# Score units taken in steps of two or three, with one sum and one reciprocal for each step

## The chip, the cores and the metric

One core of a Trainium2 chip runs the whole program. The metric is the device time of one execution in microseconds (us), lower is better. The engines are TensorE (PE in the rows; its weight loads are PEld), VectorE (DVE), ScalarE (ACT), GpSimd (POOL), and SyncE, whose queue (SP) issues the DMAs.

## The reference

Three blocks follow each other on eight batches of 576 tokens: an attention whose keys and values are pooled by 8, a gated MLP with a product over the sequence, and the block in which the change lies, four attention experts gated by their two best logits:

```python
def _moe2_ref(x, w_gate, wq, wk, wv, wo):      # x: 8 x 576 x 512, 4 experts of width 64
    logits = x @ w_gate
    topk = np.argpartition(-logits, K, axis=-1)[..., :K]          # K = 2
    ...                                                            # w: softmax over the two
    for e in range(E):
        q, k, v = x @ wq[e], x @ wk[e], x @ wv[e]
        scores = scale * (q @ k.transpose(0, 2, 1))
        scores = np.where(causal, -1000000000.0, scores)
        scores = scores - scores.max(-1, keepdims=True)
        a = np.exp(scores)
        a /= a.sum(-1, keepdims=True) + 1e-09
        ye = a @ v @ wo[e]
        ...                                                        # out += mask * w * ye
```

## The kernel before

The first two blocks (class `PhaseA`) take the first 596 us; their code does not change. The second stage (class `PhaseB`) computes the experts for one batch after the other. The four experts of a batch are two pairs `p`; the two experts `e` of a pair share tiles. The queries of a pair are cut into nine **score units** `u`: unit 0 holds the last 64 queries of both experts (`e == 2` in the table `QT`, 576 keys, in two PSUM tiles of 320 and 256 columns), units 1 to 4 are the blocks of 128 queries of the first expert with 512, 384, 256 and 128 keys, units 5 to 8 the same of the second.

A unit passes through these functions. `score`: matmuls into PSUM (L817 to L819, L829, L830), on VectorE the row maximum with the mask (L831; L822 and L824 for unit 0), on ScalarE the exponential, which also writes the row sum (L834). `scale`: on VectorE the sum plus 1e-9 (L845, L843 for unit 0) and its reciprocal (L846), both on one column, then on GpSimd (for a few units of the first and last batch on VectorE) the product of the exponentials with the reciprocal and the gate (L850). `trans`: TensorE transposes the unit (L876, L863 for unit 0), ScalarE copies the high part (L880, L867), VectorE writes the difference (L881, L872). When all units of an expert are transposed, `av` multiplies with the values (L896) in two column groups, ScalarE and VectorE fold the halves (L900, L901), and for the second expert of a pair split the result into `ah` and `al` (L906, L907), which `outp` (L918 to L920) multiplies with the output weights.

The order is written out by hand in `run`. At unit k the program issues `score(k)`, `scale(k-1)`, then the **fill** of that place, then `trans(k-3)` (`LAG = 3`), with `av` ahead of the `trans` once an expert is complete. The fill tables (`FILL`, `FIRSTF` for the first batch, `LASTF` for the last) name other work by short words: `10 11 12 13` are the four projections of pair two (two halves of q, two of k; L703 to L705), `00` to `03` those of pair one of the next batch, `v0` to `v4` its values (L757, L771 to L773), `g` its gate, `x0` to `x3` the loads of its input (L629, with casts on VectorE L630 and differences L633, L634), `o0` to `o3` the output products of the batch before. `put_q` and `put_k` copy a projection out of PSUM (L716, L718, L719, L721; L734, L735), and SyncE's queue copies parts of it to other partitions (L727 for q, L741 for k).

A scheduler then orders each engine's instructions by its own costs; the order of an engine is fixed in the program. All PSUM tiles of the stage share eight banks, `bank(name)`, in turn: a matmul into a bank waits until the tile that had it eight tiles ago has been read. Five buffers `pr` hold the exponentials in turn, and `pbh`, `pbl` one pair's transposed units.

Of the kernel before, what the change touches and what calls it, by code (L numbers as in the profile page):

```python
# [603 lines left out]
FIRSTF = (('10', '11', '12', '13', 'x0', '', 'x1 x2', 'x3', ''), ('v0 00', '', '01 02 v1', '03', '', '', '', 'v2 v3', 'v4 g'))  # L604
LASTF = (('', '10 12 11', '', '', '13', '', 'o1', '', 'o0'), ('', '', '', '', '', 'o2', '', '', 'o3'))
XV1 = (2, 3)
# [6 lines left out]
class PhaseB:  # L613
# [191 lines left out]

    def score(self, b, p, u):
        nc, w = self.nc, self.w
        i, e = QT[u]
        qs, qd, qz = self.QK["q", b, p]
        kd, kl = self.QK["k", b, p]  # L810
        st = w.tile([128, 8], F32, name="sm", bufs=4)
        pt = self.pr[:, (18 * b + 9 * p + u) % 5]
        if e == 2:
            parts = []
            for s in (slice(0, 320), slice(320, S)):
                o = self.bank("s4")[:, :s.stop - s.start]
# [5 lines left out]
            nc.vector.tensor_tensor_reduce(o, o, self.ml, -0.125, BIG, OP.add, OP.min, st[:, 4:5])  # L822
            o = parts[0][0]
            nc.vector.tensor_tensor_reduce(o, o, self.mk[:, 0:1].to_broadcast([128, 320]), -0.125, st[:, 4:5],  # L824
                                           OP.add, OP.min, st[:, 0:1])
        else:
            n = 128 * i + 128
            o = self.bank("s")[:, :n]
            nc.tensor.matmul(o, qs[:, e, 128 * i:n], kd[:, e, :n], start=True, stop=False)  # L829
            nc.tensor.matmul(o, qz[e][:, 128 * i:n], kl[:, :n], start=False, stop=True)  # L830
            nc.vector.tensor_tensor_reduce(o, o, self.mk[:, 576 - n:576], -0.125, BIG, OP.add, OP.min, st[:, 0:1])  # L831
# [3 lines left out]
        self.U[b, p, u] = (pt, st)  # L835

    def scale(self, b, p, u):
        nc = self.nc
        i, e = QT[u]
        pt, st = self.U[b, p, u]  # L840
        gw, wl = self.GW[b]
        if e == 2:
            nc.vector.tensor_scalar(st[:, 2:3], st[:, 1:2], 1e-9, st[:, 5:6], op0=OP.add, op1=OP.add)  # L843
        else:
            nc.vector.tensor_scalar(st[:, 2:3], st[:, 1:2], 1e-9, None, op0=OP.add)  # L845
        nc.vector.reciprocal(st[:, 3:4], st[:, 2:3])  # L846
        g = wl[:, p:p + 1] if e == 2 else gw[:, i, 2 * p + e:2 * p + e + 1]
        n = min(S, 128 * i + 128)
        (nc.vector if (p, u) in (SDF if b == 0 else SDL if b + 1 == B else ()) else
         nc.gpsimd).tensor_scalar(pt[:, :n], pt[:, :n], st[:, 3:4], g, op0=OP.mult, op1=OP.mult)  # L850

    def trans(self, b, p, u):
        nc, w = self.nc, self.w
        i, e = QT[u]
        pt, _ = self.U.pop((b, p, u))
        if u == 0:
# [67 lines left out]
    def run(self):  # L924
# [5 lines left out]
        vpart = lambda b: [lambda t=t: self.vproj(b, t) for t in range(NT)]  # L930
        units = [(b, p, u) for b in range(B) for p in range(2) for u in range(9)]
        def item(b, x):
            if x[0] == "x":
# [12 lines left out]
        for x in PRE.split():  # L946
            for f in item(0 if x[0] == "1" else -1, x):
                f()
        for k in range(len(units) + LAG + 1):
            if k < len(units):  # L950
                b, p, u = units[k]
                self.score(b, p, u)
            if 0 <= k - 1 < len(units):
                self.scale(*units[k - 1])
            if k < len(units):
                for x in (LASTF if b + 1 == B else FILL if b else FIRSTF)[p][u].split():
                    for f in item(b, x):
                        f()
            j = k - LAG
            if 0 <= j - 1 < len(units):  # L960
                b_, p_, u_ = units[j - 1]
                if u_ in (5, 8):
                    for g in range(2):
                        self.av(b_, p_, u_ // 8, g)
            if 0 <= j < len(units):
                self.trans(*units[j])
        for f in range(4):
# [38 lines left out]
```

## Time and profile before

| what | value |
| --- | --- |
| median of 3 runs | 986.61 us (985.52 to 988.78) |
| the profiled execution's own time | 986.47 us |
| its span | 984.4 us |
| mean granted TensorE clock | 0.979 |
| TensorE busy, share of the span | 93% |
| VectorE, ScalarE, GpSimd | 73%, 52%, 50% |

The span runs from the first to the last instruction of the profiled execution; about 2 us of its own time lie around it. Busy shares are means over both stages. In the second stage (from about 596 us) a batch repeats with the same pattern, so that stretches of a batch's length tell what a batch costs. A wait in the rows is idle time of an engine in front of an instruction, put down to the work that ended it.

### The profile page before, as it was taken

To read this page: it belongs to the slowest core of one execution; us is meant where nothing else is said; L and a number is where in the kernel's file an instruction comes from. 1 tells how busy PE (TensorE), PEld (TensorE's weight loads), DVE (VectorE), ACT (ScalarE), POOL (GpSimd) and SP (SyncE) were. 2 spreads that over 40 slices of the span, in tenths; PEclk is the share of its full clock that TensorE was granted. 3 is DMA by queue.
4 is the path that set the end of the run, shared out by engine and by line. 5 is a ranking of instruction groups with operands and counts; after the bars stand their busy time and mean duration, and the time that the engine had idled before them with its cause. 6 is when DMAs were issued, how large, how long until landed. Compare 5 with 4: busy or idle time off the path is not lost.

```text
span 984.4 us, 18357 instructions
## 1 busy us (share of the span) xinstructions
PE 915.4 (93%) x6488; PEld 863.3 (88%) x6488; DVE 715.2 (73%) x1901; ACT 511.1 (52%) x1291; POOL 490.4 (50%) x670
## 2 busy tenths in 40 slices
PE   4577899999999999999999999799999999999997
PEld 3366889989989999899899899799999999899987
DVE  6998747757567567476577524998979797979785
ACT  5576334334243343242342433576767676767776
POOL 6863727648369367375584450234434242525221
PEclk9589899999999999999999999999999999999999
DMA  9430321302302304122024012324233323322121
GB/s 331 186 101 22 101 88 47 128 26 81 110 20 71 118 12 141 45 82 99 31 62 121 1 52 70 84 48 118 72 112 72 116 74 96 84 84 84 48 60 73
DMA packets 37819, 82.92 MB, mean 84 GB/s; under 512 B 4960, under 2 KB 11104, under 8 KB 36832
## 3 DMA queue, kind: packets, MB, share of 16 engines
q1 hardware_dynamic: 37584, 81.75, 26.5%
q8 instruction: 52, 0.85, 0.4%
q14 instruction: 39, 0.32, 0.1%
q10 hardware_dynamic: 144, 0.00, 0.0%
HBM read 49.23 MB, written 18.87 MB: 69 GB/s over the span
## 4 chain that ended last, share of the span: by engine, by line
PE 57%; DVE 25%; ACT 8%; POOL 5%; issue 4%; DMA 1%; SPq 0%; POOLq 0%; ACTq 0%; DVEq 0%
PE op L445 4%; PE op L446 3%; PE op L447 3%; PE sp L420 3%; PE sp L422 3%; PE sp L421 3%; PE sc L230 3%; PE av L896 3%; DVE vnl L390 2%; DVE vnh L392 2%; ACT pr L834 2%; PE t L876 2%; PE tr L281 2%; DVE bs L376 2%; PE pj L705 2%
## 5 line engine op out<-in xcount | busy, mean ns | idle before, releaser
L850 POOL TENSOR_SCALAR pr<-pr,sm,gw 128x128 f32<-128x128 f32 (+3 forms) x119 | 77.9, 655 | 157.6 <-DVE sm L846 127.1
L834 ACT ACTIVATE pr<-s,sm 128x256 f32<-128x256 f32 (+4 forms) x160 | 83.0, 520 | 42.0 <-DVE sm L845 17.1
L332 POOL TENSOR_TENSOR xu<-x 128x576 f32<-128x576 f32 x28 | 39.2, 1428 | 98.3 <-DVE x L327 85.4
L446 PE MATMUL op<-g,woh 128*128 128x288 f32 x256 | 76.6, 301 | 4.2 <-POOL g L433 3.8
L420 PE MATMUL sp<-wsh,vnh 128*128 128x288 f32 x256 | 78.4, 306 | 1.6 <-ACT vnh L388 1.6
L404 PE MATMUL up<-x,wih 128*128 128x288 f32 x256 | 76.9, 301 | 2.4 <-ACT vg L364 2.2
L445 PE MATMUL op<-g,woh 128*128 128x288 f32 x256 | 78.2, 308 | 0.0
L421 PE MATMUL sp<-wsh,vnl 128*128 128x288 f32 x256 | 76.1, 297 | 0.0
L422 PE MATMUL sp<-wsl,vnh 128*128 128x288 f32 x256 | 75.9, 297 | 0.0
L406 PE MATMUL up<-x,wil 128*128 128x288 f32 x256 | 75.7, 296 | 0.0
L705 PE MATMUL pj<-xbh,wql 128*128 128x288 f32 x256 | 75.5, 295 | 0.0
L704 PE MATMUL pj<-xbl,wqh 128*128 128x288 f32 x256 | 75.5, 295 | 0.0
L703 PE MATMUL pj<-xbh,wqh 128*128 128x288 f32 x256 | 75.5, 295 | 0.0
L405 PE MATMUL up<-x,wih 128*128 128x288 f32 x256 | 75.1, 293 | 0.0
L447 PE MATMUL op<-g,wol 128*128 128x288 f32 x256 | 75.0, 297 | 0.0
L282 ACT ACTIVATE pth<-tr 128x640 fp32r<-128x640 f32 (+1 forms) x40 | 26.2, 654 | 79.6 <-PE tr L281 70.0
L876 PE MATMUL t<-ident,pr 128*128 128x128 f32 x320 | 57.9, 280 | 9.4 <-POOL pr L850 6.0
L831 DVE CUSTOM_DVE_ANT_0 s<-s,mk 128x512 f32<-128x512 f32 (+3 forms) x128 | 62.5, 488 | 0.4
L881 DVE TENSOR_TENSOR pbl<-t,pbh 128x512 fp32r<-128x512 f32 (+3 forms) x128 | 60.7, 484 | 2.4 <-ACT pbh L880 1.4
L230 PE MATMUL sc<-kbd,qt 128*128 128x144 f32 (+1 forms) x320 | 50.3, 303 | 10.9 <-DMA qt<-q_in 8.5
L361 PE MATMUL vp<-wih,x 128*128 128x512 f32 x128 | 52.0, 406 | 6.2 <-ACT wih L128 5.0
L896 PE MATMUL av<-pbh,vt 128*128 128x320 f32 (+4 forms) x224 | 55.6, 278 | 2.4 <-ACT pbh L880 2.4
(247 smaller groups left out, 3380.3 us busy)
## 6 DMA issues: line engine op xcount, KB each, us to landing
kraw<-k_in SPq DMA_DIRECT2D x16, 576.0 KB, 3.8
x<-x SPq DMA_DIRECT2D x32, 288.0 KB, 2.1
xb<-x SPq DMA_DIRECT2D x32, 288.0 KB, 3.0
kd<-scr SPq DMA_DIRECT2D x64, 144.0 KB, 2.5
out<-o SPq DMA_DIRECT2D x32, 288.0 KB, 2.2
vraw<-v_in SPq DMA_DIRECT2D x16, 512.0 KB, 4.1
qt<-q_in SPq DMA_DIRECT2D x7, 1152.0 KB, 6.9
st<-w_in_in SPq DMA_DIRECT2D x8, 512.0 KB, 8.9
```

The lines of the kernel that those rows point to most:

```text
L230: nc.tensor.matmul(ps[:m, p // 2, (p % 2) * 144:(p % 2) * 144 + 144], qt[:, p, o:o + m], kbd[:, p, :], start=p % 2 == 0, stop=True, skip_g ...
L420: nc.tensor.matmul(o, vh[:, k, c], self.ws[0][:, k, s], start=k == 0, stop=False)
L421: nc.tensor.matmul(o, vl[:, k, c], self.ws[0][:, k, s], start=False, stop=False)
L422: nc.tensor.matmul(o, vh[:, k, c], self.ws[1][:, k, s], start=False, stop=False)
L445: nc.tensor.matmul(o, self.wo[0][:, k, c], gh[:, s], start=k == 0, stop=False)
L446: nc.tensor.matmul(o, self.wo[0][:, k, c], gl[:, s], start=False, stop=False)
L447: nc.tensor.matmul(o, self.wo[1][:, k, c], gh[:, s], start=False, stop=k == 3)
L705: nc.tensor.matmul(ps, self.wq[1][:, kc, c], xh[:, s], start=False, stop=kc == 3)
L834: nc.scalar.activation(pt[:, s], o, AF.Exp, bias=st[:, 0:1], scale=-1.0, accum_out=st[:, 1 + 4 * j:2 + 4 * j])
L850: nc.gpsimd).tensor_scalar(pt[:, :n], pt[:, :n], st[:, 3:4], g, op0=OP.mult, op1=OP.mult)
L876: nc.tensor.transpose(ps[:, j], pt[:, 128 * j:128 * j + 128], self.ident)
L896: nc.tensor.matmul(ps[:, s - lo:], vt[:, j, 2 * p + e].rearrange("p a d -> p (a d)"), t[:, e, j * PTS + s:j * PTS + up], start=j == 0 and ...
```

## The change

The nine units of a pair are taken in four steps: units 0 and 1, 2 and 3, 4 and 5, and 6, 7 and 8. A step issues the scores of all its units, then one sum plus 1e-9 over two or three columns, one reciprocal over these columns, and the scales of all its units; then the fill of the step; then the transposes of the step before. Unit 0's two partial sums are first added by an instruction of its own. The word `a` in the fill tables is now the values product: that of the first expert of the pair before stands in a pair's first step, that of the second in its second step, each behind a projection (or a values projection). The fill tables are written anew for steps; in a middle batch the steps of pair one now carry the projections of pair two in the order k, k, then both halves of q in the third step, and the output products in the third and fourth.

```diff
-LAG = 3
-FILL = (('', '12 10 11', '', '13', 'x0', 'x1', 'o3 o1 x2 x3 o0', '', ''), ('v0', 'v1 00 02', '01 o2', '03', '', '', '', 'v2 v3', 'v4 g'))
+GROUPS = ((0, 1), (2, 3), (4, 5), (6, 7, 8))
+FILL = (('12 a', '13 a', '10 11 x0 o0', 'x1 o1 x2 o2 x3 o3'), ('v0 a v1', '02 a', '03 00 01', 'v2 v3 v4 g'))
...
-    def score(self, b, p, u):
+    def score(self, b, p, u, st, n_):
...
-        st = w.tile([128, 8], F32, name="sm", bufs=4)
+        mx = st[:, n_:n_ + 1]
...
-            nc.scalar.activation(pt[:, s], o, AF.Exp, bias=st[:, 0:1], scale=-1.0, accum_out=st[:, 1 + 4 * j:2 + 4 * j])
+            nc.scalar.activation(pt[:, s], o, AF.Exp, bias=mx, scale=-1.0,
+                                 accum_out=st[:, 13:14] if j else st[:, 3 + n_:4 + n_])
...
+    def sums(self, units, st):
+        nc, n = self.nc, len(units)
+        if QT[units[0][2]][1] == 2:
+            nc.vector.tensor_scalar(st[:, 3:4], st[:, 3:4], st[:, 13:14], None, op0=OP.add)
+        nc.vector.tensor_scalar(st[:, 6:6 + n], st[:, 3:3 + n], 1e-9, None, op0=OP.add)
+        nc.vector.reciprocal(st[:, 9:9 + n], st[:, 6:6 + n])
...
-        for k in range(len(units) + LAG + 1):
-            if k < len(units):
-                b, p, u = units[k]
-                self.score(b, p, u)
-            if 0 <= k - 1 < len(units):
-                self.scale(*units[k - 1])
...
+        for b, p, g in steps:
+            new = [(b, p, u) for u in GROUPS[g]]
+            st = self.w.tile([128, 14], F32, name="sm", bufs=3)
+            for n_, u in enumerate(new):
+                self.score(*u, st, n_)
+            self.sums(new, st)
+            for n_, u in enumerate(new):
+                self.scale(*u, st, n_)
+            for x in (LASTF if b + 1 == B else FILL if b else FIRSTF)[p][g].split():
+                for f in item(b, p, g, x):
+                    f()
+            for u in last:
+                self.trans(*u)
+            last = new
+        for u in last:
+            self.trans(*u)
+        for e in range(2):
+            for s in range(2):
+                self.av(B - 1, 1, e, s)
```

On TensorE, in pair one of a middle batch, this stood between the last matmul of the second expert's values product (`av`) and the first output product that reads its split (`op`); `t` are transposes into PSUM, `s` score matmuls:

```order
L896 MATMUL av<-pbh,vt_5926 128x64
L863 MATMUL t_7650<-ident,pr 128x128 x4
L863 MATMUL t_7657<-ident,pr 64x128
L829 MATMUL s<-kd,qs_5907 128x128
L830 MATMUL s<-qs_5907,qzvhi_5915 128x128
L876 MATMUL t<-ident,pr 128x128 x4
L829 MATMUL s<-kd,qs_5907 128x512
L830 MATMUL s<-qs_5907,qzvlo_5916 128x512
L876 MATMUL t<-ident,pr 128x128 x3
L829 MATMUL s<-kd,qs_5907 128x384
L830 MATMUL s<-qs_5907,qzvlo_5916 128x384
L918 MATMUL op<-ah,wqh 128x256
```

and this stands there now (`pj` are projections; 24 of them stand in place of the dots):

```order
L900 MATMUL av<-pbh,vt_5926 128x64
L867 MATMUL t_7552<-ident,pr 128x128 x4
L867 MATMUL t_7559<-ident,pr 64x128
L880 MATMUL t<-ident,pr 128x128 x4
L830 MATMUL s<-kd,qs_5907 128x128
L831 MATMUL s<-qs_5907,qzvhi_5915 128x128
L830 MATMUL s<-kd,qs_5907 128x512
L831 MATMUL s<-qs_5907,qzvlo_5916 128x512
L703 MATMUL pj<-xbh,wqh 128x288
...
L922 MATMUL op<-ah,wqh 128x256
```

The transposes of two units now stand together, the scores of two units behind them, and the two q projections have come between these and the output product.

On VectorE, in pair one, the units with 512 and 384 keys were followed like this, with row maxima (`ISA s,sm`, the second `ISA` reads the maximum out), the sum (`TENSOR_SCALAR sm`) and the reciprocal:

```order
L831 ISA s,sm<-s,mk 128x512
L831 ISA sm 128x1
L845 TENSOR_SCALAR sm<-sm 128x1
L881 TENSOR_TENSOR pbl<-t,pbh 128x3x128
L846 RECIPROCAL sm<-sm 128x1
L831 ISA s,sm<-s,mk 128x384
L831 ISA sm 128x1
L845 TENSOR_SCALAR sm<-sm 128x1
```

and the second step of pair one is now:

```order
L832 ISA s,sm<-s,mk 128x384
L832 ISA sm 128x1
L832 ISA s,sm<-s,mk 128x256
L832 ISA sm 128x1
L843 TENSOR_SCALAR sm<-sm 128x2
L844 RECIPROCAL sm<-sm 128x2
L735 TENSOR_TENSOR qs_5911<-pj,scr 128x288
L905 TENSOR_TENSOR scr<-av,scr 64x256
L911 TENSOR_TENSOR al<-scr,ah 128x256
L905 TENSOR_TENSOR scr<-av,scr 64x320
```

The sum before belongs to the unit in front of the one whose maximum was just taken; now it belongs to both units whose maxima stand right ahead of it.

## Rows read from the trace of the kernel before

**Rows 1.** The page's first part: busy us, share of the span, instructions.

```profile
PE 915.4 (93%) x6488; PEld 863.3 (88%) x6488; DVE 715.2 (73%) x1901; ACT 511.1 (52%) x1291; POOL 490.4 (50%) x670
```

**Rows 2.** Busy time by stretch, batches 1 to 6: stretch, length, engines, clock, DMA.

```profile
651.90:698.70 46.80, 45.38 (x349) 44.01 (x348) 40.12 (x153) 33.64 (x106) 17.92 (x24) 1.00 0.32 88
...
sum 281.10, PE 272.44 PEld 264.09 DVE 239.40 ACT 202.01 POOL 109.78; mean PE 45.41 PEld 44.01 DVE 39.90 ACT 33.67 POOL 18.30
```

**Rows 3.** Waits of TensorE's matmuls, 651 to 933 us: us, times, longest.

```profile
PE op L918 <- DVE scr L901: 4.5, 6, 0.8
PE t L876 <- POOL pr L850: 3.4, 6, 0.6
```

**Rows 4.** Waits of TensorE's weight loads, 651 to 933 us.

```profile
PEld op L918 <- DVE scr L901: 6.4, 6, 1.1
PEld t L876 <- POOL pr L850: 4.2, 6, 0.8
PEld av L896 <- DVE pbl L881: 2.3, 6, 0.4
```

**Rows 5.** Waits of TensorE's matmuls in the first batch, 608 to 651 us.

```profile
PE t L876 <- DVE pr L850: 2.6, 1, 2.6
PE t L876 <- POOL pr L850: 1.9, 3, 0.9
PE t L876 <- ACT pbh L867: 0.8, 1, 0.8
```

**Rows 6.** Waits of TensorE's matmuls in the last batch, 933 to 985 us.

```profile
PE av L896 <- ACT pbh L880: 2.4, 3, 1.0
PE t L876 <- POOL pr L850: 0.7, 1, 0.7
PE av L896 <- DVE pbl L881: 0.7, 2, 0.4
```

**Rows 7.** TensorE in order of time: start, us, instruction, count.

```profile
781.61 0.30 PE L703 MATMUL pj<-xbh,wqh 128*128 128x288 f32 x1
...
783.19 0.28 PE L896 MATMUL av<-pbh,vt 128*128 128x256 f32 x1
...
784.78 0.77 PE L863 MATMUL t<-ident,pr 128*128 128x128 f32 x5
785.30 0.31 PE L829 MATMUL s<-kd,qs 128*128 128x128 f32 x1
```

**Rows 8.** VectorE in order of time, with idle time ahead and its releaser.

```profile
775.34 0.15 DVE L845 TENSOR_SCALAR sm<-sm 128x1 f32<-128x1 f32 x1 [0.84 <-ACT pr L834]
...
805.48 1.48 DVE L630 CAST xbh<-xb 128x576 fp32r<-128x576 f32 x1
```

**Rows 9.** GpSimd in order of time.

```profile
805.22 1.42 POOL L633 TENSOR_TENSOR xbl<-xb,xbh 128x576 fp32r<-128x576 f32 x1
...
813.07 1.44 POOL L850 TENSOR_SCALAR pr<-pr,sm,gw 128x512 f32<-128x512 f32 x1 [0.59 <-DVE sm L846]
```

**Rows 10.** Groups by shape, 625 to 950 us: busy us, mean ns, idle before.

```profile
L846 DVE RECIPROCAL sm<-sm 128x1 f32<-128x1 f32 x126 | 20.4, 162 | 2.4
L831 DVE CUSTOM_DVE_ANT_0 s<-s,mk 128x512 f32<-128x512 f32 x28 | 19.3, 690 | 0.0
L834 ACT ACTIVATE pr<-s,sm 128x512 f32<-128x512 f32 x28 | 19.2, 687 | 24.9 <-DVE sm L845 15.7 <-DVE sm L831 8.2 <-DVE sm L846 1.0
L630 DVE CAST xbh<-xb 128x576 fp32r<-128x576 f32 x27 | 18.5, 684 | 0.0
L845 DVE TENSOR_SCALAR sm<-sm 128x1 f32<-128x1 f32 x111 | 16.5, 149 | 15.6 <-ACT pr L834 15.4
...
L735 DVE TENSOR_TENSOR qs<-pj,scr 128x288 fp32r<-128x288 f32 x28 | 12.8, 455 | 4.2 <-ACT scr L734 3.5
...
L901 DVE TENSOR_TENSOR scr<-av,scr 64x256 f32<-64x256 f32 x28 | 11.6, 415 | 1.4 <-ACT scr L900 1.1
```

**Rows 11.** DMA issues: KB each, median us from issue to landing.

```profile
qzvn<-qs SPq DMA_DIRECT2D x8, 128.0 KB, 2.2
```

More of the change, by code (lines that the diff above doesn't have):

```diff
@@ L821, in score @@
             o = parts[1][0].rearrange("p (a n) -> p a n", a=4)
-            nc.vector.tensor_tensor_reduce(o, o, self.ml, -0.125, BIG, OP.add, OP.min, st[:, 4:5])
+            nc.vector.tensor_tensor_reduce(o, o, self.ml, -0.125, BIG, OP.add, OP.min, st[:, 12:13])
             o = parts[0][0]
-            nc.vector.tensor_tensor_reduce(o, o, self.mk[:, 0:1].to_broadcast([128, 320]), -0.125, st[:, 4:5],
-                                           OP.add, OP.min, st[:, 0:1])
+            nc.vector.tensor_tensor_reduce(o, o, self.mk[:, 0:1].to_broadcast([128, 320]), -0.125, st[:, 12:13],
+                                           OP.add, OP.min, mx)
         else:
@@ L830, in score, with scale @@
             nc.tensor.matmul(o, qz[e][:, 128 * i:n], kl[:, :n], start=False, stop=True)
-            nc.vector.tensor_tensor_reduce(o, o, self.mk[:, 576 - n:576], -0.125, BIG, OP.add, OP.min, st[:, 0:1])
+            nc.vector.tensor_tensor_reduce(o, o, self.mk[:, 576 - n:576], -0.125, BIG, OP.add, OP.min, mx)
             parts = [(o, slice(0, n))]
         for j, (o, s) in enumerate(parts):
-            nc.scalar.activation(pt[:, s], o, AF.Exp, bias=st[:, 0:1], scale=-1.0, accum_out=st[:, 1 + 4 * j:2 + 4 * j])
-        self.U[b, p, u] = (pt, st)
-    def scale(self, b, p, u):
+            nc.scalar.activation(pt[:, s], o, AF.Exp, bias=mx, scale=-1.0,
+                                 accum_out=st[:, 13:14] if j else st[:, 3 + n_:4 + n_])
+        self.U[b, p, u] = pt
+    def sums(self, units, st):
[4 more added lines that the diff above has]
+        nc.vector.reciprocal(st[:, 9:9 + n], st[:, 6:6 + n])
+    def scale(self, b, p, u, st, n_):
         nc = self.nc
         i, e = QT[u]
-        pt, st = self.U[b, p, u]
+        pt = self.U[b, p, u]
         gw, wl = self.GW[b]
[L842 to L846, printed above, removed]
         g = wl[:, p:p + 1] if e == 2 else gw[:, i, 2 * p + e:2 * p + e + 1]
@@ L849, in scale @@
         (nc.vector if (p, u) in (SDF if b == 0 else SDL if b + 1 == B else ()) else
-         nc.gpsimd).tensor_scalar(pt[:, :n], pt[:, :n], st[:, 3:4], g, op0=OP.mult, op1=OP.mult)
+         nc.gpsimd).tensor_scalar(pt[:, :n], pt[:, :n], st[:, 9 + n_:10 + n_], g, op0=OP.mult, op1=OP.mult)
     def trans(self, b, p, u):
@@ L854, in trans @@
         i, e = QT[u]
-        pt, _ = self.U.pop((b, p, u))
+        pt = self.U.pop((b, p, u))
         if u == 0:
@@ L930, in run, with item @@
         vpart = lambda b: [lambda t=t: self.vproj(b, t) for t in range(NT)]
-        units = [(b, p, u) for b in range(B) for p in range(2) for u in range(9)]
-        def item(b, x):
+        steps = [(b, p, g) for b in range(B) for p in range(2) for g in range(4)]
+        def item(b, p, g, x):
+            if x == "a":
+                b, p = (b, 0) if p else (b - 1, 1)
+                return [lambda s=s: self.av(b, p, g, s) for s in range(2)]
             if x[0] == "x":
@@ L946, in run @@
         for x in PRE.split():
-            for f in item(0 if x[0] == "1" else -1, x):
+            for f in item(-1, 0, 0, x):
                 f()
-        for k in range(len(units) + LAG + 1):
-            if k < len(units):
-                b, p, u = units[k]
-                self.score(b, p, u)
-            if 0 <= k - 1 < len(units):
-                self.scale(*units[k - 1])
[L955 to L966, printed above, removed]
+        last = []
+        for b, p, g in steps:
[17 more added lines that the diff above has]
+                self.av(B - 1, 1, e, s)
         for f in range(4):
```

4 lines of the change are left out of this document (2 added, 2 removed).

## The prediction

> **What bounds the kernel now.** I read the page's busy shares first: TensorE is busy for 93% of the span, every other engine for 73% or less [rows 1]. That mean covers a start and two stages, so I then read the busy time by stretch over batches 1 to 6 of the second stage, the six that repeat. A batch takes 281.1 / 6 = 46.85 us. TensorE is busy for 45.41 of it and VectorE for 39.90, 85% [rows 2]; the clock is granted in full. So the stage is TensorE's, VectorE is not far behind, and the question is which 1.4 us of a batch TensorE loses, and whether the new order loses them elsewhere.
>
> The waits over these six batches answer the first half. TensorE's matmuls wait 4.5 us for the fold ahead of the output products and 3.4 us for a scaled unit that is to be transposed, once a batch each [rows 3]. Matmuls are drawn with modelled ends, so the idle time of the weight loads tells better how long nothing was fed: 6.4 us, 4.2 us, and 2.3 us in front of the values product that waits for the last difference [rows 4], together 12.9 us, 2.15 us a batch. The first batch loses 2.6 + 1.9 + 0.8 = 5.3 us in front of transposes, 2.6 of them in one piece [rows 5], the last 3.8 us [rows 6]. Those are the only places where the change can gain; the same matmuls and transposes are issued before and after.
>
> **What the change removes.** *Small VectorE work.* A batch has 18 units, so 18 sums and 18 reciprocals; now it has 8 of each and 2 additions for unit 0, 18 instructions fewer. At 0.149 and 0.162 us [rows 10] that is 18 x 0.155 = 2.8 us less on VectorE a batch. VectorE does not bound, so this counts nothing by itself; it makes room for the waits below.
>
> *The output products' wait.* Before, only twelve transposes and six score matmuls stand between the values product and the first output product, whose operand still has to be folded and split on ScalarE and VectorE. A projection of twelve matmuls takes 783.19 - 781.61 = 1.58 us, 0.13 for a matmul, and five transposes 785.30 - 784.78 = 0.52 [rows 7]; so that is 12 x 0.10 + 6 x 0.13 = 2.0 us. Now nine transposes, four score matmuls and two projections stand there, 0.9 + 0.5 + 3.2 = 4.6 us, 2.6 more against a wait of at most 1.1 [rows 4]. It goes: 6.4 us. Late next is the split of the second column group, behind the transposes' differences on VectorE, with about 1 us to spare.
>
> *The transposes' wait.* Before, a unit's transpose came three units behind its score, in the fourth quarter of a pair with little else between; the product on GpSimd was then late, 1.44 us long in the row [rows 9]. Now a unit's transposes stand behind the rest of its own step, the scores of the next step and that step's fill. The thinnest fill of a middle batch is a projection and a values product, 1.58 + (784.78 - 783.19 = 1.59) = 3.2 us [rows 7], so over 6 us lie between, against about 5 us of need: two maxima at 0.69, two exponentials at 0.69 [rows 10], sum and reciprocal 0.3, a product of 1.44 and the hand-overs. It goes: 4.2 us. The 2.3 us in front of the values product stay: it still reads the differences of the last three units right behind the next step's first work.
>
> **What it adds.** *A wait on VectorE.* The sum now stands right behind the maxima of its own step, so VectorE waits for the last exponential. Where that happened before it idled 0.84 us [rows 8]; with 8 steps a batch the upper bound is 8 x 0.84 = 6.7 us, the lower 0, where the scheduler has put a projection's difference between. Behind the sum queue the folds, the transposes' differences and the next maxima, and for these TensorE waits through the eight banks: a step writes seven to nine PSUM tiles, so a step's first score needs the tiles of the step before it read. VectorE has 39.90 - 2.8 + 6.7 = 43.8 of 46.85 us at worst, so it does not become the bound by its sum, but its backlog grows in pair one, where two splits, the gate and the casts lie.
>
> How long this backlog is I work out for the thinnest place, pair one's fourth step, whose second score takes the bank of the third step's 512-key score. Between the two TensorE has two projections, an output product of twelve matmuls, five transposes and two score matmuls: 3.2 + 1.6 + 0.5 + 0.3 = 5.6 us. That bank needs a maximum and an exponential, 0.69 each [rows 10], and 0.2 for the hand-overs: 1.6 us, once VectorE comes to it. VectorE's second step has two maxima (about 1.0 together), the wait of 0.84, a projection's difference, two folds and two splits at 0.42 to 0.46 each (2.2) [rows 8, 10], and the differences of nine transposed blocks (about 1.7 at 0.69 for four): 5.7 us, and 0.5 more where a split waits for ScalarE, against 4.6 us that TensorE's second step takes (two scores 0.6, a projection 1.58, a values product 1.59, nine transposes 0.9). If VectorE enters it some 2 us behind, after the gate and the first step's folds, it leaves it about 3.6 us behind, and the bank is free 5.2 us after its score against 5.6: 0.4 us to spare. So places like this one have next to nothing left, and one, the second step's values product, waits already. Pair two has more fill and no gate, and the backlog is gone there. The new waits lie between 0 and about 1.8 us a batch (a backlog 1 us longer turns 0.4 to spare into a wait of 0.6, at three such places); I take 0.6, nearer to the lower end where the one worked place lies: six times, 3.6 us.
>
> *The casts.* The third step's two casts follow its maxima, when GpSimd takes up the input's differences. In the row a cast that met such a difference took 1.48 us [rows 8, 9], while the mean of 27 is 0.68 [rows 10], so most of them don't meet one. [...] By the row's price for both casts the third step's backlog grows by 2 x 0.8 = 1.6 us and a batch waits about 1.6 us in place of 0.6, which would make the total 6 us longer; by the mean it stays as I have it. I stay with the mean, since the order on both engines is little changed.
>
> *The first batch.* It has no values product and no output product in pair one. The transposes that waited 5.3 us [rows 5] now have one or two projections in front and mostly stop waiting. In exchange q for pair two is projected last: between it and the scores that read its copies stand some 16 score matmuls and 10 transposes, about 16 x 0.13 + 10 x 0.10 = 3.1 us by the start-to-start times of rows 7, an estimate; the copy out of PSUM and a DMA of 2.2 us [rows 11] take as long or 1 us longer, and the next batch's input differences crowd the same place. New waits between 1 and 5 us; I take 2.5. *The last batch*: steps without projections are thin, the last step of three units is transposed with little in front of it, and the 3.8 us [rows 6] come back in other places, between 2 and 6; I take 3.8.
>
> **The sum**, against the profiled execution's own 986.5 us (span 984.4 and about 2.1 around it; the median of the runs is 986.6, the same):
> - batches 1 to 6: -6.4 - 4.2 + 3.6 = -7.0
> - first batch: -5.3 + 2.5 = -2.8
> - last batch: 0
>
> Together -9.8: **976.7 us**, 45.7 us for a middle batch. With the bounds of the new waits (0 and 10.8; 1 and 5; 2 and 6) this case reaches from 969.8 to 988.6 at its outermost, mostly 971 to 983.
>
> **Rivals.**
> *The waits move to the banks.* The exponentials, folds and differences run behind a step's scores, and each batch loses at banks and at the values product what it no longer loses at two other places: 10.6 us come back, the first batch gains 2 at most: 985. For it: the backlog of 3.6 us in pair one and the little that is to spare. Against: before, transposes and scores of four units followed each other there without a fill between, and no wait at a score stands in rows 3 or 4.
> *VectorE's queue becomes the bound* (the slower side). Its free time before was 46.85 - 39.90 = 6.95 us a batch, of which 15.6 / 6.9 = 2.3 were waits at the sums [rows 10]. If the other 4.65 us remain and every step waits its 0.84, a batch needs 39.90 - 2.8 + 6.7 + 4.65 = 48.45 us, 1.6 more than now: 6 x 1.6, and 1 more in the outer batches, give 997. It decides from the point at which VectorE's waits at sums exceed 5.1 us a batch with all other idle time kept. Against it: that idle time is mostly a wait for TensorE, which a late VectorE does not need. [...]
> *Nearly every wait goes.* Also the values product's 2.3 us, none new in the middle batches and 1 in the first: 986.5 - 10.6 - 2.3 - 4.3 - 1 = 968. For it: the small instructions that go shorten VectorE's queue just there.
>
> **How the numbers follow.** Forecast 0.58, banks 0.19, VectorE's queue 0.13, nearly every wait 0.10. No change means within 0.3%, 983.7 to 989.6, about what a measurement of this kernel can tell. Forecast and "nearly every wait" lie below that, but for a rim of the forecast that the lower rim of the banks' case outweighs: faster 0.68, same 0.19, slower 0.13. The range from 968 to 988 takes in the forecast, most of the banks' case and the edge of the best one; what is left out is the slower case and some 0.05 below. The likeliest case's own range is 971 to 983.
>
> **What would show it.** In the trace after, waits of `op` for the fold and of `t` for GpSimd should be gone from the middle batches, the values product's wait for a difference should stay near 0.4 us, VectorE should be busy some 37 us a batch with single waits of up to 0.9 us in front of the two-column sums, and a batch should repeat every 45.7 us. Waits of `s`, `pj` or `op` for an exponential or a difference of a tile eight before would show the banks; if they sum to over 1.7 us a batch I am wrong by the banks, and if VectorE idles nowhere but at sums, by its queue. Waits of pair two's scores for a DMA in middle batches would mean that q now comes too late, which I took for covered outside the first batch.

## The result, and the profile after

The changed kernel takes 992.05 us (median of 5 runs, 991.65 to 997.69) against 986.61 us for the kernel before on the same chip. The ratio is 1.0071, with a 95% interval from 1.0053 to 1.0089. It is slower by 0.7%, where 976.7 us and a gain of 1% had been forecast; the time lies outside the range.

The profiled execution of after is its slowest run, 997.69 us. Beside the profile of before, 3.3 us of that lie in the first stage, whose code is the same, so I compare stretches of the second stage. A batch is counted from its first score to the next batch's. Busy time by stretch, batches 2 to 6 of after (stretch, length, engines, clock, DMA), answers [rows 2]:

```profile
703.44:751.20 47.76, 45.49 (x349) 44.35 (x348) 38.86 (x135) 33.19 (x107) 17.09 (x25) 1.00 0.31 87
...
sum 238.77, PE 227.40 PEld 221.79 DVE 193.98 ACT 165.85 POOL 85.33; mean PE 45.48 PEld 44.36 DVE 38.80 ACT 33.17 POOL 17.07
```

A batch lasts 238.77 / 5 = 47.75 us where it lasted 46.84 in the same five before. TensorE is busy for 45.48 us of it, 45.39 before, so 0.8 of the 0.9 us are idle time. Batches 1 to 6 together went from 280.97 to 287.37 us: **+6.4 us where -7.0 were forecast**. The waits of TensorE's matmuls in these six batches (us in total, times, longest) answer [rows 3]:

```profile
PE s L830 <- DVE qs L721: 7.5, 6, 1.3
PE av L900 <- DVE pbl L885: 5.7, 6, 1.0
PE t L880 <- ACT pr L835: 0.4, 1, 0.4
```

Those of its weight loads answer [rows 4]:

```profile
PEld s L830 <- issue: 8.6, 6, 1.4
PEld av L900 <- DVE pbl L885: 6.9, 6, 1.2
PEld op L922 <- PE op L924: 1.5, 6, 0.3
PEld t L880 <- issue: 0.6, 1, 0.6
```

Both old waits are gone as forecast: the output products' 6.4 us are 1.5, of another kind, and the transposes' 4.2 us are 0.6. But once a batch a score now waits 1.25 us for a bank that a query difference (L721) must read, and the values product waits 0.95 us for the last difference (1.15 by the weight loads, which showed 0.38 a batch before). Both places lie in pair one. TensorE in order of time, batch 5:

```profile
855.54 0.39 PE L900 MATMUL av<-pbl,vt 128*128 128x256 f32 x1 [0.95 <-DVE pbl L885]
866.15 0.30 PE L830 MATMUL s<-kd,qs 128*128 128x128 f32 x1 [1.25 <-DVE qs L721]
```

I call them place A (the values product) and place B (the third score of the fourth step). What releases B is on VectorE, here in order of time:

```profile
863.69 0.45 DVE L719 TENSOR_TENSOR qs<-pj,qs 64x288 fp32r<-64x288 f32 x1
864.38 1.14 DVE L843 TENSOR_SCALAR sm<-sm 128x2 f32<-128x2 f32 x1 [0.24 <-ACT pr L835]
865.55 0.46 DVE L721 TENSOR_TENSOR qs<-pj,qs 64x288 fp32r<-64x288 f32 x1
```

GpSimd at the same time:

```profile
864.08 2.78 POOL L633 TENSOR_TENSOR xbl<-xb,xbh 128x576 fp32r<-128x576 f32 x2
```

The shared sum, an addition on two columns, lasts 1.14 us. It ends at 865.52, when GpSimd's first input difference ends (864.08 + 2.78 / 2 = 865.47). The query difference that frees the bank is queued behind it. At place A the copies of unit 0's gate weights (L802) stand between the folds and ahead of the last differences. VectorE in order of time:

```profile
852.90 0.42 DVE L905 TENSOR_TENSOR scr<-av,scr 64x256 f32<-64x256 f32 x1
853.25 0.73 DVE L802 COPY wl<-gw 64x2 f32<-64x2 f32 x2
854.01 0.48 DVE L905 TENSOR_TENSOR scr<-av,scr 64x320 f32<-64x320 f32 x1
854.42 1.07 DVE L885 TENSOR_TENSOR pbl<-t,pbh 128x384 fp32r<-128x384 f32 x3
```

GpSimd at the same time, with a scale from 853.17 to 853.96:

```profile
853.17 0.79 POOL L854 TENSOR_SCALAR pr<-pr,sm,gw 128x512 f32<-128x512 f32 x1 [3.94 <-DVE gw L799]
```

Of the two copies the first takes 0.15 us (853.25 to 853.40), although the scale has begun 0.07 us ahead of it; the second starts at 853.41 and ends at 853.98, with the scale. Why the first is not held up is open.

How long one sum, one copy and one cast lasted in the six batches of before (ns: shortest, median, longest):

```profile
L845 DVE TENSOR_SCALAR sm<-sm x96: 132/150/156, 659.1 to 933.5; 128x1 f32<-128x1 f32 x96
L802 DVE COPY wl<-gw x12: 151/158/164, 659.1 to 893.7; 64x2 f32<-64x2 f32 x12
L630 DVE CAST xbh<-xb x23: 433/492/1486, 663.7 to 906.2; 128x576 fp32r<-128x576 f32 x23
```

The same of after:

```profile
L843 DVE TENSOR_SCALAR sm<-sm x49: 160/169/1152, 655.3 to 941.8; 128x2 f32<-128x2 f32 x36, 128x3 f32<-128x3 f32 x13
L802 DVE COPY wl<-gw x12: 150/361/574, 662.2 to 901.2; 64x2 f32<-64x2 f32 x12
L630 DVE CAST xbh<-xb x23: 428/454/456, 671.8 to 917.4; 128x576 fp32r<-128x576 f32 x23
```

Before, none of the 96 sums of units 1 to 8 lasted over 156 ns and no copy over 164. 52 of these sums began while GpSimd was at work, six of them beside an input difference; none of the copies did. After, one sum in each batch lasts some 1.14 us, and one of the two copies 0.57. That makes 0.97 + 0.41 = 1.4 us of VectorE a batch, in front of the two places where TensorE waits.

In the outer batches: the first takes 42.27 us (42.39 before) at a granted clock of 0.92 (0.96 before); e13 below, the same code there, took 41.58 at 0.96. Its matmuls wait 4.1 us, 5.5 before (rows 5, and one wait of 0.2 more):

```profile
PE t L867 <- DVE pr L854: 2.5, 1, 2.5
PE s L818 <- DVE pbl L885: 0.9, 1, 0.9
PE t L880 <- POOL pr L854: 0.7, 1, 0.7
```

The last batch, from its first score to the end, takes 53.69 us, 51.76 before. Its matmuls wait 5.7 us, 3.8 before [rows 6], and the new waits lie in pair one, above all place A and an output product's bank:

```profile
PE av L900 <- DVE pbl L885: 1.0, 1, 1.0
...
PE op L922 <- ACT pr L835: 0.9, 1, 0.9
PE t L880 <- ACT qs L724: 0.6, 1, 0.6
```

### The profile page after: what moved, and what is told of

The parts are those of the page before. It is cut to its first block, busy times and chain, and to the rows that moved or that the text cites. A ratio compares the mean times of both kernels' runs of the same rounds, so it can differ in the third digit from the quotient of the medians.

```text
span 995.9 us, 18220 instructions
## 1 busy us (share of the span) xinstructions
PE 924.1 (93%) x6488; PEld 873.0 (88%) x6488; DVE 706.9 (71%) x1757; ACT 507.0 (51%) x1291; POOL 483.3 (49%) x670
## 4 chain that ended last, share of the span: by engine, by line
PE 64%; DVE 22%; ACT 6%; POOL 4%; issue 3%; DMA 1%; SPq 0%; POOLq 0%; DVEq 0%; ACTq 0%
PE av L900 4%; PE op L445 4%; PE op L446 3%; PE op L447 3%; PE sp L422 3%; PE sp L420 3%; PE sp L421 3%; PE sc L230 3%; PE t L880 3%; PE pj L703 3%; PE pj L705 3%; PE pj L704 3%; DVE vnl L390 2%; DVE vnh L392 2%; PE tr L281 2%
## 5 line engine op out<-in xcount | busy, mean ns | idle before, releaser
L854 POOL TENSOR_SCALAR pr<-pr,sm,gw 128x128 f32<-128x128 f32 (+3 forms) x119 | 73.2, 624 | 178.7 <-DVE sm L844 107.9
L885 DVE TENSOR_TENSOR pbl<-t,pbh 128x512 fp32r<-128x512 f32 (+3 forms) x128 | 58.1, 484 | 10.4 <-ACT pbh L884 9.1
L230 PEld LDWEIGHTS sc<-kbd,qt 128*128 128x128 f32 (+1 forms) x320 | 45.2, 195 | 15.1 <-issue 8.5
```

What stands on the lines that cost most here:

```text
L230: nc.tensor.matmul(ps[:m, p // 2, (p % 2) * 144:(p % 2) * 144 + 144], qt[:, p, o:o + m], kbd[:, p, :], start=p % 2 == 0, stop=True, skip_g ...
```

## The experiments

The batch is the mean of batches 2 to 6 of the profiled execution; medians and ratios are against runs of the kernel before on the same chip (986.06 to 986.61 us).

| run | median us | ratio, 95% interval | batch us |
| --- | --- | --- | --- |
| before | 986.61 | | 46.84 |
| after | 992.05 | 1.0071 (1.0053 to 1.0089) | 47.75 |
| e1 no addition of 1e-9 | 986.34 | 0.9994 (0.9985 to 1.0002) | 46.75 |
| e2 input differences swapped | 997.80 | 1.0115 (1.0100 to 1.0130) | 48.39 |
| e3 values product later | 989.76 | 1.0037 (1.0022 to 1.0052) | 47.10 |
| e4 = e1 and e3 | 987.89 | 1.0012 (1.0002 to 1.0023) | 47.13 |
| e5 query half earlier | 1001.74 | 1.0159 (1.0141 to 1.0177) | 48.13 to 50.67 |
| e6 = e1 and e5 | 1000.49 | 1.0137 (1.0112 to 1.0161) | 47.99 to 50.66 |
| e7 sums and reciprocals per unit | 993.75 | 1.0077 (1.0064 to 1.0089) | 47.54 |
| e8 before, no addition | 984.09 | 0.9982 (0.9973 to 0.9991) | 46.75 |
| e9 gate copies on GpSimd | 989.27 | 1.0029 (1.0018 to 1.0041) | 47.11 |
| e10 = e1 and e9 | 981.80 | 0.9951 (0.9932 to 0.9970) | 46.04 |
| e11 = e10, gate earlier | 982.80 | 0.9958 (0.9943 to 0.9973) | 46.49 |
| e12 before, both edits | 981.83 | 0.9957 (0.9943 to 0.9971) | 46.52 |
| e13 end of the last batch | 994.01 | 1.0075 (1.0062 to 1.0088) | 47.80 |
| e14 = e10 and e13 | 980.97 | 0.9942 (0.9923 to 0.9961) | 46.06 |
| e15 one-column additions | 989.52 | 1.0031 (1.0020 to 1.0043) | 46.78 |
| e16 = e9 and e15 | 983.89 | 0.9977 (0.9966 to 0.9987) | 46.14 |

**Place B: e1, e2, e15, e7.** e1 takes the instruction away:

```diff
-        nc.vector.tensor_scalar(st[:, 6:6 + n], st[:, 3:3 + n], 1e-9, None, op0=OP.add)
-        nc.vector.reciprocal(st[:, 9:9 + n], st[:, 6:6 + n])
+        nc.vector.reciprocal(st[:, 9:9 + n], st[:, 3:3 + n])
```

> The changed kernel without the addition of 1e-9 to the sums (a row sum is at least 1 here, so that in single precision this addition changes nothing): the reciprocal reads the sums of the exponentials directly. 50 to 60 small VectorE instructions of 0.17 us go. Theory P (the two-column addition is what holds up VectorE in the fourth step of pair one: it takes 1.13 to 1.15 us there beside GpSimd's input differences, and the query difference that frees a PSUM bank is queued behind it): the wait of the score for that bank, 1.25 us a batch by the matmuls, falls to 0.3 us or less, the batch from 47.75 to about 46.7 us, the time to about 986 us. Rival Q (VectorE's queue simply has nothing left there, and each instruction costs what it costs elsewhere): 0.17 us of the wait go, the time stays at 991 us. Rival R (the reciprocal behind it is held up in its place): the reciprocal lasts about 1.1 us, and the time is 992 us.

Theory P's numbers came: 986.34 us and a batch of 46.75. VectorE at place B in e1:

```profile
852.65 0.17 DVE L843 RECIPROCAL sm<-sm 128x2 f32<-128x2 f32 x1 [0.24 <-ACT pr L835]
852.85 0.46 DVE L721 TENSOR_TENSOR qs<-pj,qs 64x288 fp32r<-64x288 f32 x1
```

The matmuls' waits of e1 in the middle batches:

```profile
PE av L900 <- DVE pbl L885: 5.9, 6, 1.0
PE s L830 <- DVE qs L721: 1.7, 6, 0.3
```

The reciprocal, on two columns too, takes 0.17 us beside the same input difference (GpSimd starts it at 852.35), the bank wait falls from 7.5 to 1.7 us, and place A is as it was.

e2 meant to take GpSimd's work away instead:

```diff
-XV = (3,)
+XV = (0, 1)
```

> The changed kernel with the differences of the first two input loads on VectorE and those of the last two on GpSimd, so that GpSimd runs no input difference while the sum of pair one's third step waits to run; TensorE's order and VectorE's order up to the query difference are the same, and VectorE gets 1.4 us more work a batch behind it. Theory P: the sum takes 0.2 us in place of 1.14, the bank wait falls from 1.25 to 0.3 us a batch, 5 to 6 us less: 986 to 987 us, or up to 989 if the second half of the queries, now 1.4 us later, is waited for. Rival Q (queue length alone): the bank wait stays at 1.25 us, and the time is 992 us or, by the added work, up to 1 us a batch more (998).

It did not do that: one input difference stayed on GpSimd at this place, and the sum beside it was again long. VectorE in e2:

```profile
861.34 1.08 DVE L843 TENSOR_SCALAR sm<-sm 128x2 f32<-128x2 f32 x1 [0.24 <-ACT pr L835]
```

GpSimd in e2:

```profile
860.99 1.41 POOL L633 TENSOR_TENSOR xbl<-xb,xbh 128x576 fp32r<-128x576 f32 x1
```

The sum ends at 862.42, the difference at 862.40: here too the one is let go with the other. As a test of theory P against Q the run is void. It has two sums in each batch that are held up (1.06 to 1.09 us), where the changed kernel has one, and VectorE is busy for 40.6 us of a batch, 38.8 there; which of the two makes its batch longer is not shown.

e15 leaves the order at place B as it is and puts a one-column addition where the two-column one stood:

```diff
-        nc.vector.tensor_scalar(st[:, 6:6 + n], st[:, 3:3 + n], 1e-9, None, op0=OP.add)
+        for k in range(n):
+            nc.vector.tensor_scalar(st[:, 6 + k:7 + k], st[:, 3 + k:4 + k], 1e-9, None, op0=OP.add)
```

> The changed kernel with the additions of 1e-9 one column at a time and the reciprocal still over two or three columns: ten additions more a batch, and at the place in question (VectorE, third step of pair one) a one-column addition stands exactly where the two-column one stood. Theory W (only an addition over two or three columns is held up by GpSimd: in the traces all one-column additions beside GpSimd's work took 0.16 us or less, the two-column ones beside an input difference 0.29 to 1.15): this addition takes 0.15 us beside the input difference, the bank wait falls from 1.25 to 0.3 us or less, the batch from 47.75 to 46.8 us, the time to about 986 to 987 us, although VectorE has 1.5 us a batch more to do. Rival U (any addition beside the input difference is held up): 1.1 us again, 47.8 us a batch, 992 us or more.

VectorE in e15:

```profile
857.52 0.15 DVE L844 TENSOR_SCALAR sm<-sm 128x1 f32<-128x1 f32 x1
857.70 0.46 DVE L721 TENSOR_TENSOR qs<-pj,qs 64x288 fp32r<-64x288 f32 x1
```

GpSimd in e15:

```profile
857.32 2.80 POOL L633 TENSOR_TENSOR xbl<-xb,xbh 128x576 fp32r<-128x576 f32 x2
```

The matmuls' waits of e15:

```profile
PE av L901 <- DVE pbl L886: 5.6, 6, 0.9
PE s L830 <- DVE qs L721: 1.6, 6, 0.3
```

An addition on one column that started 0.2 us after GpSimd's difference was not held up (0.15 us). The batch is 46.78 us (46.8 expected), with ten additions more on VectorE; theory W holds for the two columns of this place and U falls. The runs at large say the same: in the six batches of after, e5, e9 and e13 all 24 sums on two columns that began beside an input difference lasted 0.62 to 1.15 us and ended with it, and the others, on two or three columns, lasted at most 0.17. The median of e15 is 3 us above the one expected. Beside e1's profile (985.05 us) its own (990.63) is longer by 2.2 us in the first stage, whose code is the same, and by 2.1 us in the first batch, 41.23 us at a granted clock of 0.96 against 39.10 at 1.00; what of this the ten additions cost is not told apart from the clock.

e7 also gives each unit a reciprocal of its own:

```diff
+        for k in range(n):
+            nc.vector.tensor_scalar(st[:, 6 + k:7 + k], st[:, 3 + k:4 + k], 1e-9, None, op0=OP.add)
+            nc.vector.reciprocal(st[:, 9 + k:10 + k], st[:, 6 + k:7 + k])
```

> The changed kernel, steps and tables as they are, but each unit with a sum and a reciprocal of its own again: 10 sums and 10 reciprocals more a batch, 3.4 us of VectorE. Theory P: one of the two sums of the third step still runs beside GpSimd's input difference, the two waits stay and VectorE's queue grows: batch 47.8 to 48.4 us, 992 to 996 us. Rival S (the shared sum is the cause, since the first unit of a step waits for the exponentials of the second): the scales start earlier, the waits shrink, and the time falls to 986 us or less.

The time is theory P's, and yet the bank wait is gone: no sum is held up, but another instruction. VectorE in order of time, beside two input differences of GpSimd from 859.41 to 862.43:

```profile
859.75 0.16 DVE L844 TENSOR_SCALAR sm<-sm 128x1 f32<-128x1 f32 x1
859.82 1.32 DVE L630 CAST xbh<-xb 128x576 fp32r<-128x576 f32 x1
861.06 0.15 DVE L845 RECIPROCAL sm<-sm 128x1 f32<-128x1 f32 x1
```

A cast now meets the difference, and output products wait (3.1 + 1.3 us in the six batches). The 3.1 us are not the cast's: they end with ScalarE's copy of an output (L926), which starts at 860.37 behind other work of ScalarE, while the cast lasts until 861.14. What else makes them wait is open. So theory P, as I had put it for this run (one of the two sums is still held up), was wrong; rival S was right about the bank and wrong about the time.

**Place A: e3, e4, e9, e10, e11.** e3 moves the values product:

```diff
-FILL = (('12 a', '13 a', '10 11 x0 o0', ...
+FILL = (('12 a', '13', 'a1 10 11 x0 o0', ...
```

> The changed kernel with the second values product of pair one moved from behind the projection in the second step to the start of the third step's fill: in front of it now stand the transposes of units 0 and 1 and the two scores of the third step. Theory A (the values product waits 0.95 to 1.0 us a batch for the difference of unit 8, which VectorE writes late): the wait goes, because some 2.5 us of TensorE work stand between; the batch falls from 47.75 to 46.7 us, the time to about 986 us. Rival (the wait has a twin): the transposes of units 0 and 1, now 2.9 us earlier, wait for GpSimd's scales, or the folds, now later, hold up the query evacuations and the bank wait grows from 1.25 us to 2 us and more; the time stays at 990 to 993 us.

> The changed kernel with both edits, no addition of 1e-9 and the second values product in the third step. If the two waits are two causes, the gains add up: batch about 45.7 us, the time about 980 us. If both are one shortage of VectorE that moves from place to place, the sum is no more than the larger of the two: 985 to 987 us.

Both waits went in e3, at B too, since in its order no sum ran beside an input difference (the longest took 0.17 us), but a third appeared; the matmuls' waits of e3:

```profile
PE t L867 <- POOL pr L854: 4.0, 6, 0.7
PE op L922 <- ACT ah L910: 3.2, 6, 0.6
PE op L924 <- DVE al L911: 1.8, 6, 0.3
```

The transposes now wait for the scales and the output products for the split: a twin, as the rival had it, at 0.65 us a batch less. With nothing held up at B any more, e4 could add nothing to the batch (47.13).

e9 only moves the two copies to GpSimd:

```diff
-            nc.vector.tensor_copy(wl[64 * h:64 * h + 64], gw[:64, 4, h::2])
+            nc.gpsimd.tensor_copy(wl[64 * h:64 * h + 64], gw[:64, 4, h::2])
```

> The changed kernel with the two tiny copies of unit 0's gate weights (wl, 64x2) on GpSimd in place of VectorE; sums and tables as in the changed kernel. In the changed kernel's trace these two copies take 0.73 us a batch on VectorE right ahead of the last differences of pair two, where in the trace before they took 0.32 us, and one of the two lies beside a scale of GpSimd. Theory A (the values product waits for a difference that stands behind the gate's work on VectorE): its wait falls from 0.95 us to 0.2 to 0.45 us a batch, the other wait (the bank) stays: batch from 47.75 to about 47.2 us, about 989 us. Rival (ScalarE's copies of the high parts end only just ahead of these differences and set them): the wait stays, 992 us. Rival (GpSimd's copies delay its scales): the transposes wait in turn, 992 us or more.

> The changed kernel without the addition of 1e-9 and with the two gate copies on GpSimd. If the two waits are two causes, the gains add up: batch from 47.75 to 46.2 us, the time about 983 us, below the kernel before. If the wait only moves on, as in the runs with the values product or the query half moved, 986 us.

The matmuls' waits of e9:

```profile
PE s L830 <- DVE qs L721: 7.5, 6, 1.3
PE av L900 <- DVE pbl L885: 1.8, 6, 0.3
```

Those of e10:

```profile
PE av L900 <- DVE pbl L885: 1.8, 6, 0.3
PE s L830 <- DVE qs L721: 1.7, 6, 0.3
```

In e9 place A falls from 5.7 to 1.8 us and B stays to the digit; in e10 both shrink. The batches: 47.75, less 1.00 for the sum (e1) and 0.64 for the copies (e9), would be 46.11; e10 has 46.04. **They are two causes, and they add up.** The 1.00 us are those of the held-up sum, since e15 gains 0.97 with the sums still there. The 0.64 us are those of the copies as a whole: e9 takes the 0.41 us of the hold-up and the 0.32 us of the copies themselves out of VectorE's queue together, and no run parts them.

> As the run before, and with one values projection (the third token block of the next batch) moved from pair two's fourth step to its second, so that the gate's chain on VectorE begins a projection (1.7 us of TensorE) earlier against the next batch's first scores, ahead of which it stands. Theory A: the rest of the wait at the values product goes too, batch 45.8 to 46.0 us, about 981 us. Rival (no slack left in pair two's second step either): a wait of 0.3 to 0.8 us a batch appears there, 983 to 987 us.

e11 moved a projection from one step to another (`'02 a v2', '03 00 01', 'v3 v4 g'`). Place A's matmul wait went but for one of 0.3 us, and one of 0.5 us a batch came at the transposes, for an exponential: the rival.

**Moving the query half: e5, e6.** (`'12 a', '13 10 a', '11 x0 o0'`)

> The changed kernel with one word of the middle batches' table moved: the first half of pair two's query projection stands in the second step, between k's second half and the values product, in place of the third step. The sums stay as they are. Theory A and P together (two places without slack: the values product that waits for unit 8's difference, and the score that waits for the bank of this query half behind the held-up sum): 12 matmuls, 1.5 us of TensorE, now stand ahead of the values product, and the bank is read some 5 us earlier, so both waits go: batch from 47.75 to about 45.6 us, the time to 979 us. Rival (moving work only moves the wait, as when the values product was moved): one of the two goes and an equal one comes at the transposes or at the output products, the batch is 46.7 us, the time 986 us.

> As the run before, and also without the addition of 1e-9. If the earlier query half has taken the bank wait away, the held-up sum lies behind nothing that TensorE waits for, and this changes the batch by less than 0.2 us (about 978 us). If the sum still holds up something, 1 us a batch more goes (about 973 us or, when the earlier query half only moved a wait, 980 us).

Worse than any theory. A and the old B went, but with one projection fewer between them the same score now takes the bank of a score of the step before (unit 5's, 512 keys) and waits for its exponential. The matmuls' wait in e5:

```profile
PE s L830 <- ACT pr L835: 5.8, 6, 1.0
```

Busy time and granted clock around that score in one batch, by stretches of 3 us (columns as in [rows 2]):

```profile
860.21:863.21 3.00, 2.49 (x15) 1.67 (x13) 2.94 (x7) 0.83 (x4) 0.86 (x1) 1.00 0.32 88
863.21:866.21 3.00, 1.97 (x8) 1.62 (x9) 2.24 (x8) 2.90 (x10) 2.44 (x3) 0.72 0.43 100
866.21:869.21 3.00, 3.00 (x14) 3.00 (x14) 2.94 (x12) 2.08 (x9) 2.21 (x4) 0.50 0.87 254
869.21:872.21 3.00, 3.00 (x18) 3.00 (x17) 1.20 (x5) 1.48 (x5) 1.96 (x4) 0.64 0.39 148
```

Behind the wait the granted clock falls from 1.00 to 0.72, 0.50 and 0.64 in the next three stretches. If it was 0.50 wherever it was low, that is (0.28 + 0.50 + 0.36) x 3 / 0.5 = 6.8 us in all, an estimate from these rows. Such batches take 49.5 to 50.7 us, the others, where the same wait stands and the clock stays at 1.00, 48.1. An undisturbed batch is still 0.4 us longer than after's, with TensorE busy 0.8 us more (46.31 against 45.49 us); why, I leave open. That e6 changes an undisturbed batch by some 0.1 to 0.15 us fits a sum that no longer stands before a wait.

**The order before, with the same edits: e8, e12.**

> The kernel before without the addition of 1e-9 (unit 0 keeps the addition of its two parts): 16 additions of 0.15 us go in each batch, and none of them lasted over 0.16 us in its trace. Theory P (the addition costs something only where GpSimd's input difference holds it up, and here it never does): TensorE's waits hardly change, the batch stays within 0.3 us, 985 to 987 us. Rival Q (VectorE's queue has nothing left anywhere, so that 2.4 us fewer of it a batch count): 1 us a batch or more, 980 us or less.

> The kernel before with the same two edits (no addition of 1e-9 for units 1 to 8, the gate copies on GpSimd). In its trace the copies took 0.16 us each, never held up. Theory (both edits pay only where GpSimd's work holds VectorE's small instructions up): within 0.2 us a batch of the run without the addition alone, 983 to 985 us. Rival: the edits are worth the same in any order, 981 us or less.

Without the addition the batch changes by 0.1 us; rival Q (1 us or more) falls, though the time is 0.9 us below the range given. e12 is 2 us faster still, 0.23 us a batch, near the rival: 0.32 us of copies ahead of the differences cost something here too, though nothing held them up. With both edits on both sides the two orders take the same time, 981.80 and 981.83 us, though the changed one has batches shorter by 0.5 us. By the profiles of e10 and e12 batches 1 to 6 take 276.7 and 279.2 us, and the last batch 54.3 and 51.3: what the order gains in the middle it loses at the end, there at a granted clock of 0.97 against 1.00.

**The last batch: e13, e14** move the values product of the last pair's first expert ahead of the transposes of units 6 to 8.

> The changed kernel with one move behind the last step: the values product of the last pair's first expert ahead of the transposes of units 6 to 8, where the changed kernel has both values products behind them. Theory T (the last batch lost 2.0 us, since the last three transposes stand alone and wait 2.2 us for scales and copies, where the kernel before had this values product beside them): the last batch loses 1.3 to 2 us less, the time falls from 992.05 to about 990.4 us; batches 1 to 6 stay at 47.75 us. Rival (the products only change places, and the wait comes behind the transposes, at the second expert's values product): within 0.5 us of 992.

> The same move in the kernel without the addition of 1e-9 and with the gate copies on GpSimd (981.8 us without the move, equal to the kernel before with the same two edits, although its batches are 0.5 us shorter). Theory T (what its batches win is lost in the last batch): about 980 us, below the kernel before with both edits (981.8). Rival: 981.5 to 982 us, and what its shorter batches win is lost elsewhere.

Theory T falls: the waits for scales stay (0.84 and 0.42), and in place of one of 0.91 us for a copy two of 0.39 and 0.78 come at the values products; from pair two's first score to the last matmul's start it is 29.51 us (957.89 to 987.40), 29.14 without the move (962.92 to 992.06). What the last batch loses stays read from the waits above, not tested.

**The whole computation, without hold-ups: e16.**

> As the run before, and with the two gate copies on GpSimd: nothing is left out of the computation. Theory W: both hold-ups are gone and the gains add up: 46.1 us a batch, 982 to 983 us. Rival (the ten additions more on VectorE's queue count where it had little left): 46.5 us a batch or more, 985 us.

46.14 us a batch as expected, and 983.89 us, 1 us more than expected: nothing left out and 0.23% below the kernel before. By the weight loads its six batches wait 6.7 us, near the 5.9 that the prediction left (2.3 and 3.6), though a batch is still 0.4 us longer than the 45.7 forecast. So the hold-ups, and not the order of the steps, are what made the batches longer: with the same edits on both sides the new order's are the shorter ones (46.04 us in e10, 46.52 in e12). The fastest are e14 and e10 (980.97 and 981.80, intervals overlapping), whose reciprocal reads the sum without 1e-9.

## Why the prediction was wrong

- *The two old waits.* Right: 10.6 us by the weight loads, of which 2.1 are left at these instructions.
- *Small VectorE work.* **This is the step that failed.** I counted the 18 instructions fewer "at 0.149 and 0.162 us", and the ones left at that price too, but the row is for one column. The shared addition has another price: on two columns it was held up beside GpSimd's input difference (1.14 us), on one it was not (0.15 us in e15). Sharing made the sum cost 1.14 us once a batch, where it stands before the bank that TensorE waits for. I had forecast 37 us of VectorE a batch; it is 38.80, 1.8 more, and 1.4 us of VectorE are hold-ups of the sum and of a copy that the forecast did not have.
- *The new waits, "between 0 and about 1.8 us a batch", of which "I take 0.6".* By the weight loads (the rows above and one of 0.3 us) they are (17.9 - 2.3) / 6 = 2.6, above the upper end. That the fourth step's scores and the second step's values product had nothing left was right, though the wait came at the third score, behind a query difference, and not at the second, which I had worked out; what tipped them, 1.0 and 0.64 us a batch (e1, e9), was not in the sum. The rival "the waits move to the banks" (985 us; over 1.7 us a batch) comes nearest in kind, though its sign is not there (place B has 1.25 us a batch) and its mechanism, a backlog of exponentials and folds, is not what the runs show; the queue rival's 997 us needed idle time at the sums of over 5.1 us a batch, and it is (14.9 + 7.3) / 5 = 4.4.
- *"The 2.3 us in front of the values product stay."* Wrong: 1.15 for 0.38 by the weight loads. I followed its own differences and not the gate's copies, one of which is now held up beside a scale.
- *The casts.* I weighed the row's 1.48 us beside a difference for the casts alone, and then stayed with the mean "since the order on both engines is little changed". For the casts that came out better than the mean, and for a reason that I had not seen: before, one cast in each batch lasted 1.48 us beside GpSimd's difference, after, none over 0.46 (the rows on sums, copies and casts above). In both orders one VectorE instruction in each batch is held up beside the difference, and now it is the sum, behind which TensorE waits. The trace shows this of the sum and of a copy beside a scale: 1.14 and 0.57 us, each ending with GpSimd's instruction; the first of the two copies, 0.15 us beside the same scale, was not held up. Nor was an addition on a single column, in e15 and e7 (0.15 and 0.16 us). What in the hardware makes the one wait for the other is not shown; the runs show the columns and the common end.
- *First and last batch.* -2.8 forecast, about -0.8 measured at an equal clock (42.39 to 41.58 in e13): the transposes' wait of 2.5 us for a scale stayed. 0 forecast, +1.9 measured, with place A and two more waits in pair one.

In sum: +6.4, -0.8 and +1.9 are +7.5 us by the profiles, within the interval of the runs (+5.2 to +8.8). What the last batch loses was not found by an experiment. The chance of 0.13 for slower was too low because the only slower rival was a queue, and none was an instruction that changes its price with its shape.

## What to carry to other kernels

When instructions are merged, look up the price of the merged shape, not of the old one: beside GpSimd's input difference an addition on one column took 0.15 us (e15), on two columns it lasted until the difference ended, 1.14 us (after). Price a reorder by what stands beside each small VectorE instruction ahead of a wait, and put copies that only GpSimd's work needs on GpSimd (0.64 us a batch in e9). Moving work around a wait brought a twin wait four times out of four (e3, e5, e11, e13); taking the held-up instruction out of the queue paid where TensorE waited behind it (e1, e9, e10), and not where it did not (e4, e6).

## What the hardware showed that I had not expected

- A VectorE addition of 128x2 lasted up to 1.15 us in place of 0.17 beside GpSimd's difference of 128x576 (1.41 us), a copy of 64x2 0.57 in place of 0.16 beside a scale of 128x512 (0.79 us); one-column additions (at most 0.16 us, before, e15 and e7) and reciprocals (0.17, e1) beside the difference were not held up.
- Of two copies of 64x2 beside one scale of GpSimd only the second was held up (0.57 us, the first 0.15), in all six batches.
- The copy of 64x2 takes 0.18 us on GpSimd (e10), against 0.16 on VectorE (before); the input difference 1.41 (after) against 0.76 (e3).
- Behind the same wait of 1 us the granted clock fell to 0.50 in some batches of e5 and stayed at 1.00 in others.
